# A spectral filter and gated MLP on one core: the late row blocks' last transform as three rounded products, with its operands split one step ahead

## The chip, the cores and the metric

One core of one Trainium2 chip runs one program. The metric is the device time in microseconds. Three runs of the kernel before took 457.14, 457.20 and 456.63 us, median 457.14 us. Besides these there is one profiled execution, whose trace gives the start, the end and the releaser of the instructions on each engine: PE (matrix products; PEld is its loading of stationary operands), DVE and POOL (elementwise), ACT (elementwise and activation functions) and SP, which here issues all the data transfers. Lines such as L956 are those of the kernel before.

## What is computed

The input `x` has 2048 rows of 512 values. Two residual steps follow each other: a filter in the frequency domain, and a gated MLP with 1376 hidden units.

```python
def _A_ref(x, w_r, w_i):                       # global filter
    X = jnp.fft.rfft2(x, axes=(-2, -1)) * (w_r + 1j * w_i)
    return jnp.fft.irfft2(X, s=(S, D), axes=(-2, -1))

def _B_ref(x, w_gate, w_up, w_down):           # gated GELU
    h = gelu(x @ w_gate) * (x @ w_up)
    return h @ w_down

h = x + _A_ref(layernorm(x), w_r, w_i)
out = h + _B_ref(layernorm(h), w_gate, w_up, w_down)
```

All data is 32-bit floating point.

## The kernel before

**The transforms are products.** The 2048 rows are held as 16 row blocks `b` of 128 rows (row 16p + b lies on partition p). The two-dimensional transform is split into products with small constant matrices: over the 128 partitions (`mf`, and `mi` on the way back, kept in SBUF as `mis`), over the 16 blocks (`cf`, `ci`), and over the 512 columns (`df`, `di`). `gh` is the large buffer [128, 16, 512] that holds the spectrum on its way back and then the residual stream `h`. The way back for a block `b` is: over the columns (`over_d_back`, L510, four 128-wide products), a fold of the four column quarters into whole rows (`unfolded`, L805, four POOL instructions of 256 columns, L809 to L812), and then *over the rows*: one product of `mis[:, b]` (128x128) with the block's 512 columns, written to a PSUM bank. The residual `x - mean` is added while the bank is emptied (L957), and the second layer norm's statistics follow (`stats2`, L502).

**Two kinds of products.** A product of two 32-bit operands, as at L956, appears in the trace as two PE records. The MLP instead uses *rounded* operands (type `fp32r`): `split` (L91) writes the rounded value `hi` by an ACT copy (L93) and the rest `lo = full - hi` by a subtraction (L94) on DVE or another engine, and `mm3` (L96) forms hi·hi + hi·lo + lo·hi by three products into one bank (L100, L101, L102).

**The MLP.** Pairs of row blocks are combined so that a 2x2 block product takes seven products instead of eight (`combine`, L530; `products`, L610). Rows come in two halves `q`: blocks 0 to 7, then 8 to 15. For each half the hidden units are walked in eleven *tiles* `n` of 128 units. A tile (`gate_up`, L694) runs the products P0 to P6 into three PSUM banks (banks 0 to 2 or 3 to 5 by the parity of `n`), each of two `mm3`, so six PE products of 512 columns. ACT and DVE empty the banks around them (L651, L654), apply the GELU (L657), multiply gate and up (L660) and split the result into `a` (L666 on ACT for `hi`, L673 on DVE for `lo`). `load_gu` (L127) prepares the next tile's weights: a transfer into `raw`, sums on POOL (L138 to L146), the rounded cast on DVE (L153) and the rests on POOL (L156, three pieces of 256, 768 and 768 columns). `load_d` (L489) does the same for the down weights (L494 on ACT, L496 on POOL). `down` (L732) multiplies `a` with the down weights into banks 6 and 7 (L747), which alternate, and DVE adds each into `gh` (L753, in the last group L750).

**What sets the order.** In the phase `FIRST` (L34, run at L940) the order on PE, ACT, DVE and POOL is written out by hand: blocks 0 to 7 go all the way (`whole`, L814), blocks 8, 9 and 12 (`BY_THEN`) go up to their unfolding, the pairs of the first half are normalised and combined, and tiles 0 and 1 are computed in halves of 256 columns. From tile 2 on (L978) only PE's order is written out. For ACT, DVE, POOL and SP a scheduler places the instructions at build time by a model of time, so an instruction that the source names late may be placed far ahead, among those of `FIRST` too. Each engine then runs its instructions strictly in that order; one that waits holds up all behind it.

**The late blocks.** The generator `late(b)` (L946) has two steps. The first unfolds block `b` on POOL, behind the last L156 (`held("lo")`), except for blocks 8, 12 and 9. The second loads the block's rows of `x`, takes the next of banks 6 and 7, runs the product over the rows on PE (L956), and adds the residual and takes the statistics on DVE. The first step of the blocks listed in `lates` is called near the end of tile `n`: blocks 9 and 13 at tile 2, 10 at tile 3, 14 at tile 4, 11 at tile 5, 15 at tile 6. The second is called in the next tile, after its products P1 and P2. Blocks 8 and 12 get their second step in tile 2.

Of the kernel before, what the change touches and what calls it, by code (L numbers as in the profile page):

```python
# [13 lines left out]
F32R = mybir.dt.float32r  # L14
# [5 lines left out]
S, D, F = 2048, 512, 1376  # L20
P = 128
# [36 lines left out]
def kernel(  # L58
# [15 lines left out]
    nc = tc.nc  # L74
    pe, act, dve, pool = nc.tensor, nc.scalar, nc.vector, nc.gpsimd
# [4 lines left out]
    gh = base.tile([P, NB, D], F32, name="gh")  # L80
# [10 lines left out]
    def split(hi, lo, full, eng=dve):  # L91

        act.activation(hi, full, AF.Copy)  # L93
        eng.tensor_tensor(lo, full, hi.bitcast(F32), op=ALU.subtract)  # L94

    def mm3(o, pairs, onto=False):  # L96

        n = len(pairs)
        for i, ((lh, ll), (rh, rl)) in enumerate(pairs):
            pe.matmul(o, lh, rh, start=(i == 0 and not onto), stop=False, skip_group_check=True)  # L100
            pe.matmul(o, lh, rl, start=False, stop=False, skip_group_check=True)  # L101
            last = pe.matmul(o, ll, rh, start=False, stop=(i == n - 1), skip_group_check=True)  # L102
        return last
# [6 lines left out]
    mis = k3.tile([P, NB, P], F32, name="mis")  # L110
# [12 lines left out]
    def held(k):  # L123

        return tc.issue_after(pooled[k].ins) if k in pooled else ExitStack()

    def load_gu(f, slowly=False, after=None):  # L127

        nonlocal turn
        t = wgp.tile([P, 7, 2 * P], F32, name="raw")  # L130
        nc.sync.dma_start(t[:, :2], wgu[f, :, :2])
        nc.sync.dma_start(t[:, 3:6:2], wgu[f, :, 2:])
        r = gus[:, turn]
        turn = 1 - turn
        gu[f] = r.rearrange("p h m (c n) -> p h m c n", c=2)
        yield
        with held("late"):
            i = pool.tensor_tensor(t[:, 4], t[:, 0], t[:, 3], op=ALU.subtract)  # L138
        if after:
            behind(i, after())  # L140
        yield
        pool.tensor_tensor(t[:, 3], t[:, 3], t[:, 5], op=ALU.add)
        yield
        pool.tensor_tensor(t[:, 2], t[:, 3], t[:, 0], op=ALU.subtract)
        yield
        pool.tensor_tensor(t[:, 6], t[:, 1], t[:, 2], op=ALU.subtract)  # L146
        yield
        if slowly:
            for m in range(7):
                split(r[:, 0, m], r[:, 1, m], t[:, m], pool)  # L150
                yield
        else:
            dve.tensor_copy(r[:, 0], t)  # L153
            yield
            for m in (slice(0, 1), slice(1, 4), slice(4, 7)):
                pooled["lo"] = pool.tensor_tensor(r[:, 1, m], t[:, m], r[:, 0, m].bitcast(F32), op=ALU.subtract)  # L156
                yield
# [328 lines left out]
    w3 = ctx.enter_context(tc.tile_pool(name="w3", bufs=2, reuse_waits="tile"))  # L486
# [12 lines left out]
    def row():  # L499
        return rp.tile([P, D], F32, name="row")  # L500

    def stats2(b):  # L502

        bn = w3.tile([P, 32], F32, name="bn")[:, :6]
        dve.bn_stats(bn, gh[:, b])
        yield
        dve.bn_aggr(mv2[:, b], bn)
        yield
# [92 lines left out]
    def in_turn(i, hns, banks):  # L601

        do = combine(i, hns)
        places = {"T0": ps[:, banks[0]], "T1": ps[:, banks[1]], "s": row(), "e": row()}
        for names in ("T0 a b", "T1 s c d e f g h k", "i j l m n o"):
            for k in names.split():
                do[k](*[places[k]] if k in places else [])
            yield
# [85 lines left out]
    def gate_up(n):  # L694

        do = products(n)[1] if n == 2 else tile_of(n)

        def all_of(names):
            for k in names.split():
                ins = do[k]()  # L700
            return ins

        all_of("P0")
        if n == 2:

            yield
            do = tile_of(n)
            all_of("c1 P1 d1")
        else:
            all_of("c1")  # L710
            yield
            all_of("P1 d1")
        yield
        for names in ("P2 c2", "P3"):
            all_of(names)
            yield
        last = copied[n] = all_of("P4 c3")
        all_of("dy")
        yield

        for _ in load_d(tiles[n][1], last):
            pass

        for names in ("P5", "P6 d2"):
            all_of(names)
            k = names[1] == "6"
            with tc.issue_after(last.ins):
                do[f"G{k:d}"]()
            all_of(f"m{k:d} i{k:d} o{k:d}")
            yield  # L730
# [74 lines left out]
    def unfolded(b, v):  # L805

        s4, v4 = (a.rearrange("p (e h n) -> p e h n", e=2, h=2) for a in (gh[:, b], v))
        u = gh[:, b].rearrange("p (e n) -> p e n", e=2)
        pool.tensor_tensor(v4[:, :, 0], s4[:, :, 0], s4[:, :, 1], op=ALU.add)  # L809
        pool.tensor_tensor(v4[:, :, 1], s4[:, :, 0], s4[:, :, 1], op=ALU.subtract)  # L810
        pool.tensor_tensor(u[:, 0], v[:, :256], v[:, 256:], op=ALU.add)
        pooled["late"] = pool.tensor_tensor(u[:, 1], v[:, :256], v[:, 256:], op=ALU.subtract)  # L812
# [115 lines left out]
    def step(n):  # L928

        if n not in begun_tiles:  # L930
            f = tiles[n][1]
            if f not in gu:
                for _ in load_gu(f):
                    pass
            begun_tiles[n] = gate_up(n)
        next(begun_tiles[n])
# [9 lines left out]
    def late(b):  # L946

        if b not in BY_THEN:

            with held("lo"):  # L950
                unfolded(b, row())
        yield
        xt = row()
        nc.sync.dma_start(xt, x3[:, b])
        py = ps[:, next(bank_67)]
        pe.matmul(py, mis[:, b], gh[:, b], start=True, stop=True)  # L956
        dve.scalar_tensor_tensor(gh[:, b], xt, mv[:, b, 0:1], py, op0=ALU.subtract, op1=ALU.add)  # L957
        for _ in stats2(b):
            pass
        yield  # L960

    def normed(b):

        hn = row()
        act.activation(hn, gh[:, b], AF.Copy, scale=rs2[:, b : b + 1])
        return hn

    def fill(n):
        for _ in range(n):
            next(downs, None)  # L970


    lates = {2: (9, 13), 3: (10,), 4: (14,), 5: (11,), 6: (15,)}
    ending = [late(b) for b in BY_THEN[:2]]
    for g in ending:
        next(g)
    downs = down(0, orders[0][:2], False)
    with tc.manual_schedule(engines={et.PE}):  # L978
        for n, (q, f) in list(enumerate(tiles))[2:]:
            k, at_change = n - q * NF, n == NF - 1  # L980
            if k == 0:
                step(n)
            step(n)
            if k > 8 and not q:
                for i in range(2 * k - 18, 2 * k - 16):
                    with tc.issue_after(copied[n - 1].ins):
                        hns[i] = [normed(b) for b in (8 + i, 12 + i)]
            step(n)
            if at_change:

                steps = [in_turn(i, hns[i], banks) for i, banks in enumerate(((3, 4), (5, 0), (3, 4), (1, 2)))]
                next(steps[0])
            for g in ending:
                next(g)
            if n in (6, 7):

                norm_scales(2 * n - 4, 2)
            fill(2)
            step(n)
            fill(2)  # L1000
            step(n)
            fill(2)

            if k == NF - 1:
                downs = down(q, orders[q][-3:], True)
            if at_change:
                next(steps[0])
                next(steps[1])
            elif k < NF - 1:
                step(n + 1)  # L1010
                fill(2)
            else:
                fill(1)
            ending = [late(b) for b in lates.get(n, ())]
            for g in ending:
                next(g)
            step(n)
            step(n)
            if k in (4, 7):
                downs = down(q, orders[q][: k + 1][-3:], False)  # L1020
            elif k == 1:
                downs = down(q, orders[q][:2], False)
            if at_change:
                gu = {f: gu[f] for f in orders[0][-2:]}
                for s in steps:
                    for _ in s:
                        pass
                    fill(2)
            if k == NF - 1:
                fill(12)  # L1030
# [125 lines left out]
```

## Time and profile before

| what | value |
| --- | --- |
| median of three runs | 457.14 us (456.63 to 457.20) |
| the profiled execution | 456.41 us |
| its span, first to last instruction | 454.6 us |
| PE clock granted | 0.999 |
| instructions in the trace | 6435 |
| packets on the hardware transfer queue | 21136, 40.64 MB |

The profiled execution's own time is 1.8 us above its span. A busy time is the sum of the records of an engine, and PE records overlap: a product of 512 columns has a record of 0.39 us while the next starts 0.23 us later. In the chain of waits the time of a product is what it adds to the chain. In a row of the timeline, the first two numbers are the start in the span and the duration, and the bracket at the end tells how long the engine had been idle and which instruction released it. `x2` or `x12` means that so many equal instructions were merged into one row.

### The profile page before, as it was taken

How to read it: one execution, taken by the hardware profiler on the slowest of the kernel's cores; microseconds unless marked ns; L12 is line 12 of the kernel's file. 1: busy time of each engine (PE TensorE's matmuls, PEld its weight loads, DVE VectorE, ACT ScalarE, POOL GpSimd, SP SyncE). 2: the span in 40 equal slices, each digit the busy share in tenths (PEclk: the TensorE clock that was granted, in tenths of full speed). 3: DMA queues.
4: the chain of work that ended last, by engine and by line, in shares of the span. 5: the costliest groups of instructions: out<-in, count | busy, mean ns of one | idle time of the engine just before them, and what ended most of it. 6: DMA issues, size and time to landing. Idle time of an engine off the chain costs nothing.

```text
span 454.6 us, 6435 instructions
## 1 busy us (share of the span) xinstructions
PE 438.9 (97%) x2289; PEld 371.4 (82%) x2289; DVE 276.9 (61%) x513; ACT 206.6 (45%) x433; POOL 275.5 (61%) x305
## 2 busy tenths in 40 slices
PE   3999998999999999999999999999999999999997
PEld 3899998788967777887888888888888888888876
DVE  5966986797665676358744579256565355535453
ACT  3979876688751233024422776242243024302420
POOL 5985996968868578828752744155566536663210
PEclk9999999999999999999999999999999999999999
DMA  8994804300031122112210203131022102210013
GB/s 253 399 406 132 284 32 156 123 25 1 25 115 47 48 92 92 48 47 71 69 46 25 70 25 128 57 85 55 25 70 69 48 24 71 69 46 25 23 66 121
DMA packets 21168, 41.05 MB, mean 90 GB/s; under 512 B 2064, under 2 KB 7696, under 8 KB 21008
## 3 DMA queue, kind: packets, MB, share of 16 engines
q1 hardware_dynamic: 21136, 40.64, 26.2%
q8 instruction: 18, 0.29, 0.3%
q14 instruction: 14, 0.11, 0.1%
HBM read 36.44 MB, written 4.19 MB: 89 GB/s over the span
## 4 chain that ended last, share of the span: by engine, by line
PE 89%; ACT 4%; DVE 2%; DMA 2%; issue 1%; SPq 1%; DVEq 0%; ACTq 0%
PE ps L747 26%; PE ps L100 15%; PE ps L102 15%; PE ps L101 15%; PE ps L416 3%; PE ps L515 3%; PE ps L427 3%; PE ps L448 2%; PE ps L288 2%; DMA gh<-in_x 2%; PE ps L848 1%; PE ps L956 1%; PE ps L554 1%; ACT ts L293 1%; PE ps L548 1%
## 5 line engine op out<-in xcount | busy, mean ns | idle before, releaser
L100 PE MATMUL ps<-cb,gu 128*128 128x512 f32 (+1 forms) x336 | 127.8, 380 | 2.0 <-ACT s L651 1.6
L747 PE MATMUL ps<-wd,a 128*128 128x512 f32 (+1 forms) x537 | 126.1, 388 | 0.2 <-DVE gh L750 0.2
L102 PE MATMUL ps<-cb,gu 128*128 128x512 f32 (+1 forms) x336 | 124.9, 372 | 0.0
L101 PE MATMUL ps<-cb,gu 128*128 128x512 f32 (+1 forms) x336 | 124.8, 371 | 0.0
L747 PEld LDWEIGHTS ps<-wd,a 128*128 128x128 f32 x537 | 99.2, 188 | 22.4 <-DVE gh L957 0.9
L156 POOL TENSOR_TENSOR gu<-raw,gu 128x768 fp32r<-128x768 f32 (+1 forms) x54 | 78.2, 1476 | 40.0 <-DVE gu L153 38.7
L651 ACT ACTIVATE s<-ps 128x512 f32<-128x512 f32 (+1 forms) x72 | 40.4, 561 | 134.4 <-PE ps L102 134.2
L100 PEld LDWEIGHTS ps<-cb,gu 128*128 128x128 f32 x336 | 63.2, 188 | 15.0 <-ACT s L651 2.2
L101 PEld LDWEIGHTS ps<-cb,gu 128*128 128x128 f32 x336 | 63.2, 188 | 11.7 <-issue 1.0
L102 PEld LDWEIGHTS ps<-cb,gu 128*128 128x128 f32 x336 | 63.2, 188 | 11.1
L753 DVE TENSOR_TENSOR gh<-ps,gh 128x512 f32<-128x512 f32 x48 | 33.0, 690 | 53.5 <-PE ps L747 53.4
L496 POOL TENSOR_TENSOR wd<-wdr,wd 128x512 fp32r<-128x512 f32 x22 | 28.5, 1295 | 51.5 <-ACT wd L494 51.5
L660 DVE TENSOR_TENSOR ps<-ps,s 128x512 f32<-128x512 f32 (+1 forms) x48 | 31.0, 649 | 24.8 <-PE ps L102 22.5
L666 ACT ACTIVATE a<-ps 128x512 fp32r<-128x512 f32 (+1 forms) x48 | 26.9, 561 | 39.0 <-DVE ps L660 38.6
L673 DVE TENSOR_TENSOR a<-ps,a 128x512 fp32r<-128x512 f32 (+1 forms) x48 | 30.7, 640 | 11.8 <-ACT a L666 10.4
L138 POOL TENSOR_TENSOR raw<-raw 128x256 f32<-128x256 f32 x20 | 14.7, 737 | 37.8 <-DMA raw<-in_wgu 36.7
L654 DVE TENSOR_TENSOR s<-ps,s 128x512 f32<-128x512 f32 (+1 forms) x48 | 30.8, 642 | 10.3 <-PE ps L102 8.7
L657 ACT ACTIVATE s<-s 128x512 f32<-128x512 f32 (+1 forms) x48 | 28.2, 592 | 18.4 <-DVE s L654 18.4
L654 DVE TENSOR_TENSOR ps<-ps,s 128x512 f32<-128x512 f32 (+1 forms) x24 | 15.7, 654 | 27.7 <-ACT s L651 27.7
L288 PE MATMUL ps<-ms,pn 128*128 128x128 f32 x120 | 17.6, 297 | 8.3 <-ACT ms L256 8.1
L288 PEld LDWEIGHTS ps<-ms,pn 128*128 128x128 f32 x120 | 16.1, 210 | 8.8 <-POOL pn L263 8.8
L153 DVE CAST gu<-raw 128x1792 fp32r<-128x1792 f32 x18 | 19.6, 1091 | 4.5 <-PE ps L101 2.9
(124 smaller groups left out, 609.7 us busy)
## 6 DMA issues: line engine op xcount, KB each, us to landing
raw<-in_wgu SPq DMA_DIRECT2D x40, 256.0 KB, 3.1
wt<-in_w SPq DMA_DIRECT2D x16, 520.0 KB, 5.4
wdr<-in_wd SPq DMA_DIRECT2D x22, 256.0 KB, 2.6
out<-gh SPq DMA_DIRECT2D x15, 256.0 KB, 2.0
gh<-in_x SPq DMA_DIRECT2D x7, 512.0 KB, 9.6
row<-in_x SPq DMA_DIRECT2D x12, 256.0 KB, 3.0
mis<-in_mi SPq DMA_DIRECT2D x1, 1024.0 KB, 10.7
a<-in_x SPq DMA_DIRECT2D x4, 256.0 KB, 4.3
```

Source lines behind the costliest of these rows:

```text
L100: pe.matmul(o, lh, rh, start=(i == 0 and not onto), stop=False, skip_group_check=True)
L101: pe.matmul(o, lh, rl, start=False, stop=False, skip_group_check=True)
L102: last = pe.matmul(o, ll, rh, start=False, stop=(i == n - 1), skip_group_check=True)
L156: pooled["lo"] = pool.tensor_tensor(r[:, 1, m], t[:, m], r[:, 0, m].bitcast(F32), op=ALU.subtract)
L288: pe.matmul(pt[:, c], o, mc, start=(z == 0), stop=(z == len(parts[b][c]) - 1))
L496: pool.tensor_tensor(r[:, 1], t, r[:, 0].bitcast(F32), op=ALU.subtract)
L651: return lambda: act.activation(to, a, AF.Copy)
L654: return lambda: dve.tensor_tensor(to, a, b, op=ALU.add)
L660: return lambda: dve.tensor_tensor(u, u, g, op=ALU.mult)
L673: dve.tensor_tensor(a[:, 1], u, a[:, 0].bitcast(F32), op=ALU.subtract)
L747: pe.matmul(o, parts_of[tiles.index((q, f))][:, ha, i // 4, r], wds[f][:, hw, c], start=start, stop=stop)
L753: dve.tensor_tensor(gh[:, b, c], o, gh[:, b, c], op=ALU.add)
```

## The change

A step is put between the two steps of `late(b)`: it allocates two tiles from the pool `w3` (two buffers of each), `m` for the two halves of `mis[:, b]` and `v` for those of `gh[:, b]`, and splits both, with an ACT copy and a DVE subtraction each. The product over the rows becomes an `mm3` of these. The main loop calls the new step after a tile's P1, and the product, as before, after its P2. The scratch area that the program reserves for transfers is set to 4096 bytes, where nothing was given before.

```diff
             with held("lo"):
                 unfolded(b, row())
         yield
+        m = w3.tile([P, 2, P], F32R, name="m")
+        v = w3.tile([P, 2, D], F32R, name="v")
+        split(v[:, 0], v[:, 1], gh[:, b])
+        split(m[:, 0], m[:, 1], mis[:, b])
+        yield
         xt = row()
         nc.sync.dma_start(xt, x3[:, b])
         py = ps[:, next(bank_67)]
-        pe.matmul(py, mis[:, b], gh[:, b], start=True, stop=True)
+        mm3(py, [((m[:, 0], m[:, 1]), (v[:, 0], v[:, 1]))])
         dve.scalar_tensor_tensor(gh[:, b], xt, mv[:, b, 0:1], py, op0=ALU.subtract, op1=ALU.add)
...
             if k == 0:
                 step(n)
             step(n)
+            for g in ending:
+                next(g)
             if k > 8 and not q:
...
-    nc = bacc.Bacc("TRN2", target_bir_lowering=False, num_devices=1)
+    nc = bacc.Bacc("TRN2", target_bir_lowering=False, num_devices=1, dynamic_dma_scratch_size=4096)
```

What the scheduler makes of it, in the built program: the order on SP is the same, on POOL one L138 and one L496 change places. The splits of `m` for blocks 8 and 12 stand on ACT behind the last L450 and ahead of the first L830, and on DVE ahead of the first L838, before `FIRST` begins its work. The splits of `v` for blocks 8 and 12 stand inside the end of `FIRST`: on ACT between an L657 and an L666, on DVE between an L654 and an L673. The others stand near their blocks; that of `v` for block 14 is placed on ACT between an L657 and an L651, and on DVE between an L660 and an L673. The splits of `m` for a later block follow the products that free the buffer, which puts them next to the L957 (L962 in the changed kernel) of an earlier block.

## The prediction

> **What bounds the kernel now.** I read the page from the top: busy times, then the chain of waits, then a table of the stretches in which the changed lines run.
>
> ```profile
> span 454.6 us, 6435 instructions
> ...
> PE 438.9 (97%) x2289; PEld 371.4 (82%) x2289; DVE 276.9 (61%) x513; ACT 206.6 (45%) x433; POOL 275.5 (61%) x305
> ...
> PE 89%; ACT 4%; DVE 2%; DMA 2%; issue 1%; SPq 1%; DVEq 0%; ACTq 0%
> 130.00:160.00 30.00, 29.93 (x125) 22.70 (x125) 20.00 (x35) 7.68 (x15) 19.97 (x21) 1.00 0.23 72
> 160.00:190.00 30.00, 30.00 (x130) 24.10 (x129) 17.13 (x28) 9.35 (x17) 24.58 (x28) 1.00 0.25 87
> ```
>
> TensorE is busy 97% of the span and carries 89% of the chain. In the two stretches that hold most of the late row blocks (columns: PE, PEld, DVE, ACT, POOL busy) PE has no gap, DVE is busy half to two thirds of the time, ACT a quarter to a third. So a microsecond of PE work saved there, or of PE waiting added, goes straight into the time. Other engines cost something only where PE, directly or through a queue, waits for them. The clock column stays at 1.00.
>
> **The gain: products.** Per late block, two records of one 32-bit product are replaced by three rounded products.
>
> ```profile
> L956 PE MATMUL ps<-gh,mis 128*128 128x512 f32 x16 | 7.8, 591 | 0.0
> 125.48 0.39 ACT s L651
> 125.92 0.38 PE ps L100
> 134.15 0.76 DVE gh L957
> 134.95 3.06 PE ps L747 x12
> 139.39 3.02 PE ps L747 x12
> 156.00 1.72 PE ps L956 x4
> 157.72 0.23 PE ps L100
> 177.72 0.86 PE ps L956 x2
> ```
>
> Records overlap, so what one adds is read from the chain: 1.72 us for the four of two blocks, 0.43 each, 0.86 a block. A rounded product of this width adds 0.227 (0.23 in the chain; twelve L747 in 2.72 us unstalled). Three add 0.68, so 0.18 is saved per block: 8 x 0.18 = **-1.46 us**. [...]
>
> **The cost: operands.** Each block now issues two copies on ACT (L93: `m` 128x128, `v` 128x512) and two subtractions on DVE (L94).
>
> ```profile
> L494 ACT ACTIVATE wd<-wdr 128x512 fp32r<-128x512 f32 x22 | 13.7, 625 | 8.2 <-PE ps L747 8.2
> L480 ACT ACTIVATE nis<-mis 128x128 f32<-128x128 f32 x2 | 0.5, 300 | 0.0
> L505 DVE BATCH_NORM_STATS2 bn<-gh 128x6 f32<-128x512 f32 x16 | 10.9, 682 | 0.0
> L156 POOL TENSOR_TENSOR gu<-raw,gu 128x768 fp32r<-128x768 f32 x36 | 65.7, 1845 | 0.0
> 14.87 1.26 POOL L263 TENSOR_TENSOR pn<-gh 128x512 f32<-128x512 f32 x1
> 15.14 1.54 DVE L277 TENSOR_TENSOR uv<-pn 128x512 f32<-128x512 f32 x1
> 16.10 1.72 POOL L262 TENSOR_TENSOR pn<-gh 128x512 f32<-128x512 f32 x1
> 29.70 0.42 DVE L277 TENSOR_TENSOR uv<-pn 128x256 f32<-128x256 f32 x1
> 74.22 1.86 POOL L94 TENSOR_TENSOR gu<-raw,gu 128x256 fp32r<-128x256 f32 x2
> 74.34 1.16 DVE L438 TENSOR_TENSOR z<-t,t 128x520 f32<-128x520 f32 x1
> 75.53 0.57 DVE L440 TENSOR_TENSOR z<-z 128x2 f32<-128x2 f32 x1
> ```
>
> ACT: 0.62 + 0.30 a block, 7.4 us over the run, into its idle time. DVE alone would need 0.68 and, on the slope from 0.42 at 256 to 0.68 at 512, some 0.29: 7.8 us. But these read both operands from SBUF, and such a DVE instruction does not run beside a POOL one here. L277 arrives 0.27 into POOL's L263 and ends 0.55 after it (16.68 against 16.13); the POOL instruction behind it then takes 1.72 instead of 1.26. L440, a 2-wide addition right behind L438, takes 0.57, since POOL's second L94 went in between (it ends at 76.08, L440 at 76.10): the two alternate. So a split costs DVE its own 0.55 after the POOL instruction in flight, and POOL about 0.45. POOL instructions are up to 1.85 long and POOL is busy two thirds to four fifths of these stretches.
>
> **Where it decides: the end of the hand-written order.** By the program order, the splits of `v` for blocks 8 and 12 stand on DVE between an L654 and the L673 that follows it; on ACT their copies stand before an L666, and a later L666 waits for that L673.
>
> ```profile
> 123.94 0.42 DVE L654 TENSOR_TENSOR s<-ps,s 128x256 f32<-128x256 f32 x1
> 124.17 2.52 POOL L156 TENSOR_TENSOR gu<-raw,gu 128x256 fp32r<-128x256 f32 x2 [2.16 <-DVE gu L153]
> 124.27 0.41 DVE L673 TENSOR_TENSOR a<-ps,a 128x256 fp32r<-128x256 f32 x1
> 124.72 0.38 ACT L666 ACTIVATE a<-ps 128x256 fp32r<-128x256 f32 x1 [0.30 <-DVE a L673]
> ```
>
> Before, L673 (124.27) releases ACT's L666 (124.72), behind it L657 and L651 (125.48), and that L651 releases PE (125.92, the second row of the chain above). Nothing in it is slack. The two subtractions now come first. POOL's first L156 (0.74; the row's two pieces are 256 and 768 wide) starts at 124.17, 0.10 before the first subtraction can. So: subtraction of 8 ends 124.91 + 0.55 = 125.46; the second L156 goes in between and ends 1.845 - 0.13 later, 127.18 (L262 above ended 1.14 after L277, 0.13 under the 1.27 of its kind); subtraction of 12 ends 127.73; L673 starts 0.09 before that, at 127.64 instead of 124.27. **+3.37 us** for PE at 125.92. What follows hangs on PE, or on ACT's queue behind this L651 (L494, then POOL's L496, L156 and the weight load), so it moves along and pays nothing back. Bounds: +1.2 if the port costs nothing (two steps of 0.60), +1.75 if DVE keeps the port for both, 3.4 if they alternate; I take the last, which L440 shows.
>
> [...]
>
> **The other places** (clock of before, the shift left out).
>
> ```profile
> 136.27 0.74 POOL L146 TENSOR_TENSOR raw<-raw 128x256 f32<-128x256 f32 x1
> 137.05 1.09 DVE L153 CAST gu<-raw 128x1792 fp32r<-128x1792 f32 x1 [0.68 <-POOL raw L146]
> 138.66 1.27 DVE L753 TENSOR_TENSOR gh<-ps,gh 128x512 f32<-128x512 f32 x2
> 161.16 0.70 DVE L654 TENSOR_TENSOR ps<-ps,s 128x512 f32<-128x512 f32 x1 [0.72 <-ACT s L651]
> 175.99 0.76 POOL L812 TENSOR_TENSOR gh<-row 128x256 f32<-128x256 f32 x1
> 177.00 0.69 DVE L660 TENSOR_TENSOR ps<-ps,s 128x512 f32<-128x512 f32 x1
> ```
>
> Tile 2: PE restarts at 139.39 when L753 frees a bank, so DVE sets the pace. New ahead of it are the split of `v` for block 9 and of `m` for 9 and 13, and they hold up POOL's L144 and L146 by 0.45 and 0.2, for whose end (137.01) L153 waits. L153 starts near 138.4; the second L505 now stands ahead of it, so L753 follows 1.0 behind, at 139.4 instead of 138.66. PE is 0.74 late where it should be 0.37 early: **+1.11** (0.2 without the port).
>
> Tile 3: a split of `m` meets the last L156 of 1.85 and the L654 of 161.16 slips to about 162.3, its end to 163.0. PE's product that accumulates onto the same bank (P6) follows 24 products of 0.227 after the 157.72 of the chain, so it starts at 163.0 (a start lies 0.16 before its place in the chain), and at 162.6 once the two blocks' 0.36 are saved: **+0.36** (0 to 1).
>
> Tile 5: block 14 is unfolded by POOL until 176.75, and its first product was issued at 177.56 (0.16 before the chain's 177.72) and is now due 0.18 earlier with block 10's saving. Now the copy must lie between (0.62) and the subtraction behind it, after L660 (177.69) and against POOL's next instructions. With 0.3 for POOL's own delay, the high half is ready at 177.67, the low half at 178.35 to 179.1, the second product's turn is 177.61: **+1.1** (0.7 to 1.5). Behind the copy, which now waits for POOL on ACT, stands the L651 that empties PE's bank; it was not due before 177.8 and loses nothing.
>
> Blocks 10, 11 and 15 have their rows some 4 us ahead or more; their splits fall into DVE's idle time: nothing, at worst 0.5 each. The splits of `m` for 8 and 12 stand between the last L450 and the first L830:
>
> ```profile
> 77.41 0.60 ACT L450 ACTIVATE gh<-ps 128x512 f32<-128x512 f32 x1 [1.11 <-PE ps L448]
> 79.26 0.60 ACT L830 ACTIVATE row<-ps 128x512 f32<-128x512 f32 x1 [1.25 <-PE ps L515]
> q1 hardware_dynamic: 21136, 40.64, 26.2%
> ```
>
> 1.25 us idle on ACT cover 0.6; without that cover it would cost PE the 0.6. SP's order of transfers is unchanged (the load of `row` is issued where it was); on POOL one L138 and L496 change places, for nothing. All data moves through the hardware queue that SP feeds, so the smaller scratch moves addresses and costs nothing.
>
> **Sum**: -1.46 + 3.37 + 1.11 + 0.36 + 1.1 = +4.5 us. The profiled execution took 456.41 us (span 454.6, 1.8 around it), so 460.9; the runs' median is 457.14, 0.7 above it, so **461.6 us**, 460.2 to 463.2 by the bounds of these terms.
>
> **The rivals.**
> - All hidden, the side of a gain: DVE, idle a third of the time, takes the splits in its gaps and only the products show. 457.14 - 1.46 = 455.7. For it: after the L673 of 124.27 DVE has little to do until PE is back. Against: its gaps lie behind that L673, which is what ACT waits for.
> - No port: SBUF subtractions run beside POOL. Then 1.2 at 124, 0.2 in tile 2, 0.6 in tile 5: -1.46 + 2.0 = +0.5, 457.7. Against it L277 and L440.
> - One wait only: DVE keeps the port for both splits, or the first gets it ahead of POOL. 4.5 - 3.37 + 1.75 = +2.9, 460.0. For it: the margin is 0.10 us.
>
> **How the numbers follow.** Forecast 0.56, one wait 0.16, no port 0.13, all hidden 0.15. A measurement tells 0.2% (0.9 us) from no change. Faster 0.15; within 0.2% 0.10 (most of the third case); slower 0.56 + 0.16 + 0.03 = 0.75. The range reaches from below the third case to the top of the first: 457.4 to 463.2; it leaves out the first rival and little above.
>
> **What would show it.** The two L94 of DVE near 124 to 128 with 1.2 and over 2 us instead of 0.68, an L673 behind them near 127.6, PE idle over 3 us before the L100 that stood at 125.92, released by ACT's L651. Three v products per block 0.68 apart from what follows. POOL's L156 lengthened next to L94. PE waits before L747 at the start of tile 2 and before L101 of block 14. I am wrong if the L94 of `v` take 0.68 beside a busy POOL, or if PE has no new gap near 126.

## The result, and the profile after

The changed kernel took 462.47 us (median of 6 runs, 460.15 to 464.32), the kernel before beside it 456.88 us (456.38 to 457.36): 1.0116 times, with a 95% interval of 1.0088 to 1.0143. It is slower by 5.6 us; the forecast was 461.6 us. The profiled execution was the fastest of the six: 460.15 us with a span of 458.4, so the trace explains 3.7 of the 5.6 us.

The page of the changed kernel, its span, busy times and the shares of the chain of waits:

```profile
span 458.4 us, 6478 instructions
...
PE 439.2 (96%) x2297; PEld 374.1 (82%) x2297; DVE 289.6 (63%) x529; ACT 213.0 (46%) x449; POOL 278.3 (61%) x305
...
PE 71%; POOL 12%; ACT 6%; issue 3%; DMA 3%; DVE 3%; SPq 1%; POOLq 0%; ACTq 0%
```

PE is busy 0.3 us longer than before, in a span 3.8 longer. The chain now runs over POOL for 12% (it had no share in the line before), ACT 6 and DVE 3%: waits of other engines have entered it.

The timeline of the changed kernel at the end of the hand-written order, in order of time (start, duration, engine; behind the row, the idle time before it and who ended it):

```profile
124.14 2.95 POOL L156 TENSOR_TENSOR gu<-raw,gu 128x256 fp32r<-128x256 f32 x2 [2.16 <-DVE gu L153]
124.25 3.39 DVE L94 TENSOR_TENSOR v<-gh,v 128x512 fp32r<-128x512 f32 x2
127.56 0.41 DVE L673 TENSOR_TENSOR a<-ps,a 128x256 fp32r<-128x256 f32 x1
128.00 0.38 ACT L666 ACTIVATE a<-ps 128x256 fp32r<-128x256 f32 x1 [3.60 <-DVE a L673]
128.59 0.38 ACT L651 ACTIVATE s<-ps 128x256 f32<-128x256 f32 x1
129.02 0.39 PE L100 MATMUL ps<-cb,gu 128*128 128x256 f32 x1 [3.59 <-ACT s L651]
130.60 0.63 PE L100 MATMUL ps<-cb,gu 128*128 128x512 f32 x1
```

This is the forecast link by link: two subtractions of `v` in 3.39 us instead of 1.2, POOL's two pieces in 2.95 instead of 2.52, L673 at 127.56 (forecast 127.64), and behind it ACT and TensorE. The product that stood at 125.92 starts at 129.02. The last row was not in the forecast: a 512-wide product has a record of 0.63 us instead of 0.39. The table of stretches shows why (columns: PE, PEld, DVE, ACT, POOL busy, then the granted clock, then the DMA share and GB/s):

```profile
128.00:129.00 1.00, 0.00 (x0) 0.00 (x0) 0.42 (x1) 0.99 (x4) 0.00 (x0) 1.00 0.00 0
129.00:130.00 1.00, 0.98 (x7) 0.98 (x8) 0.00 (x0) 0.76 (x2) 0.16 (x1) 1.00 0.00 0
130.00:131.00 1.00, 1.00 (x5) 0.74 (x4) 0.93 (x3) 0.00 (x0) 1.00 (x1) 0.73 0.00 0
131.00:132.00 1.00, 1.00 (x4) 0.68 (x3) 0.60 (x2) 0.00 (x0) 1.00 (x2) 0.50 0.00 0
132.00:133.00 1.00, 1.00 (x7) 1.00 (x6) 0.00 (x0) 0.89 (x3) 0.91 (x1) 0.50 0.54 199
133.00:134.00 1.00, 1.00 (x7) 1.00 (x7) 0.98 (x3) 0.47 (x2) 0.00 (x0) 0.56 0.26 72
134.00:135.00 1.00, 1.00 (x8) 0.91 (x8) 0.85 (x4) 0.73 (x3) 0.00 (x0) 1.00 0.77 219
```

Behind the idle time the granted clock is 0.50 in the slices from 131 to 133 and 1.00 before 130 and behind 134. If it was at one of these two values throughout, 0.73 in one slice and 0.56 in another put the half clock between 130.46 and 133.88, 3.42 us.

**A ruler for the stages.** TensorE's order is the same in all these kernels (a few products are moved in the later ones, 13 are added in one), and up to 22 us behind the first gate product (the first L100 on `cb,gu`) their traces agree to 0.02 us. So each stage can be measured as the start of a TensorE row minus the start of that product, without what lies ahead of it, which differs from execution to execution. Two rows of the timeline of TensorE, kernel after:

```profile
97.86 0.47 PE L100 MATMUL ps<-cb,gu 128*128 128x256 f32 x1
137.16 0.39 PE L100 MATMUL ps<-v,m 128*128 128x512 f32 x1
```

Block 8 starts 137.16 - 97.86 = 39.30 us behind it; before it was 133.03 - 97.89 = 35.14, so +4.16. In the same way, as differences to the kernel before (us; e1 to e9 are the experiments below, "end" is the rest of the span):

| start of | before | after | e7 again | e2 only 8, 12 | e1 8, 12 old | e3 behind | e5 POOL waits | e6 warm | e8 moved |
| --- | --- | --- | --- | --- | --- | --- | --- | --- | --- |
| block 8's products | 35.14 | +4.16 | +4.01 | +4.16 | 0.00 | +0.01 | +1.00 | +3.15 | +0.01 |
| blocks 9 and 13 | 57.95 | +4.22 | +4.39 | +3.66 | +0.32 | +0.36 | +1.66 | +3.72 | -0.45 |
| block 10 | 69.24 | +3.87 | +4.06 | +3.65 | 0.00 | +0.01 | +1.34 | +3.37 | -0.79 |
| block 14's place | 79.67 | +3.85 | +4.04 | +3.65 | -0.03 | -0.02 | +1.29 | +3.33 | -1.02 |
| block 11 | 106.41 | +4.28 | +4.45 | +3.66 | +0.41 | +0.42 | +1.73 | +3.76 | -1.24 |
| block 15 | 116.84 | +4.05 | +4.22 | +3.65 | +0.18 | +0.19 | +1.49 | +3.53 | -1.47 |
| L747 behind block 15 | 127.27 | +3.82 | +4.00 | +3.65 | -0.06 | -0.04 | +1.27 | +3.30 | -1.70 |
| end | 356.71 | +3.83 | +3.99 | +3.68 | -0.08 | -0.04 | +1.32 | +3.24 | -1.74 |
| first gate product at | 97.89 | 97.86 | 98.70 | 100.71 | 101.67 | 99.53 | 99.17 | 99.55 | 98.93 |

How fine the ruler is, two kernels below say that leave these products and splits as they were: e4 and e11 agree with the kernel before up to block 8 and stand 0.14 and 0.17 us under it from tile 2 on, to within 0.06. Both have the smaller scratch, so whether this is the scratch or the spread of the executions is not told. So tile 2 is known to some 0.15 us, the other stages better; the row "end" goes by spans that are printed to 0.1 us.

A block in which nothing is late shows its gain alone: block 11 takes +4.28 to +4.05, block 15 the same step, -0.23 each. Where a step is smaller, the difference is what the place cost. If a block's own first product is late, that shows in the step before it (block 14, below).

### The profile page after: what moved, and what is told of

Its sections match the earlier page's. It is cut to its first block, busy times and chain, and to the rows that moved or that the text cites. A ratio compares the mean times of both kernels' runs of the same rounds, so it can differ in the third digit from the quotient of the medians.

```text
span 458.4 us, 6478 instructions
## 1 busy us (share of the span) xinstructions
PE 439.2 (96%) x2297; PEld 374.1 (82%) x2297; DVE 289.6 (63%) x529; ACT 213.0 (46%) x449; POOL 278.3 (61%) x305
## 4 chain that ended last, share of the span: by engine, by line
PE 71%; POOL 12%; ACT 6%; issue 3%; DMA 3%; DVE 3%; SPq 1%; POOLq 0%; ACTq 0%
PE ps L747 23%; PE ps L100 12%; PE ps L101 12%; PE ps L102 12%; PE ps L288 4%; POOL gu L156 3%; PE ps L515 3%; POOL z L438 2%; ACT dp L420 2%; DMA raw<-in_wgu 2%; DMA gh<-in_x 2%; PE ps L848 1%; DVE v L94 1%; PE ps L554 1%; POOL wd L496 1%
## 5 line engine op out<-in xcount | busy, mean ns | idle before, releaser
L100 PE MATMUL ps<-cb,gu 128*128 128x512 f32 (+1 forms) x336 | 126.6, 377 | 4.9 <-ACT s L651 4.7
L747 PE MATMUL ps<-wd,a 128*128 128x512 f32 (+1 forms) x537 | 125.7, 387 | 0.7 <-DVE gh L753 0.3
L747 PEld LDWEIGHTS ps<-wd,a 128*128 128x128 f32 x537 | 99.3, 188 | 22.0 <-DVE gh L753 0.8
L156 POOL TENSOR_TENSOR gu<-raw,gu 128x768 fp32r<-128x768 f32 (+1 forms) x54 | 78.8, 1488 | 40.0 <-DVE gu L153 37.6
L651 ACT ACTIVATE s<-ps 128x512 f32<-128x512 f32 (+1 forms) x72 | 40.4, 561 | 117.8 <-PE ps L102 117.5
L100 PEld LDWEIGHTS ps<-cb,gu 128*128 128x128 f32 x336 | 63.5, 189 | 17.0 <-ACT s L651 5.3
L496 POOL TENSOR_TENSOR wd<-wdr,wd 128x512 fp32r<-128x512 f32 x22 | 28.5, 1293 | 53.7 <-ACT wd L494 53.7
L666 ACT ACTIVATE a<-ps 128x512 fp32r<-128x512 f32 (+1 forms) x48 | 26.9, 561 | 40.9 <-DVE ps L660 37.3
L660 DVE TENSOR_TENSOR ps<-ps,s 128x512 f32<-128x512 f32 (+1 forms) x48 | 31.0, 650 | 22.9 <-PE ps L102 20.6
L673 DVE TENSOR_TENSOR a<-ps,a 128x512 fp32r<-128x512 f32 (+1 forms) x48 | 30.7, 640 | 12.5 <-ACT a L666 11.2
L138 POOL TENSOR_TENSOR raw<-raw 128x256 f32<-128x256 f32 x20 | 15.2, 760 | 37.0 <-DMA raw<-in_wgu 35.9
L657 ACT ACTIVATE s<-s 128x512 f32<-128x512 f32 (+1 forms) x48 | 28.2, 592 | 19.0 <-DVE s L654 19.0
L654 DVE TENSOR_TENSOR s<-ps,s 128x512 f32<-128x512 f32 (+1 forms) x48 | 30.8, 642 | 9.5 <-PE ps L102 8.0
L654 DVE TENSOR_TENSOR ps<-ps,s 128x512 f32<-128x512 f32 (+1 forms) x24 | 15.6, 652 | 24.1 <-ACT s L651 24.1
L288 PE MATMUL ps<-ms,pn 128*128 128x128 f32 x120 | 17.6, 297 | 8.2 <-ACT ms L256 8.0
L288 PEld LDWEIGHTS ps<-ms,pn 128*128 128x128 f32 x120 | 16.1, 210 | 8.6 <-issue 8.6
L153 DVE CAST gu<-raw 128x1792 fp32r<-128x1792 f32 x18 | 19.6, 1090 | 4.3 <-PE ps L101 3.0
```

The lines of the kernel that those rows point to most:

```text
L288: pe.matmul(pt[:, c], o, mc, start=(z == 0), stop=(z == len(parts[b][c]) - 1))
L496: pool.tensor_tensor(r[:, 1], t, r[:, 0].bitcast(F32), op=ALU.subtract)
L651: return lambda: act.activation(to, a, AF.Copy)
L654: return lambda: dve.tensor_tensor(to, a, b, op=ALU.add)
L660: return lambda: dve.tensor_tensor(u, u, g, op=ALU.mult)
L673: dve.tensor_tensor(a[:, 1], u, a[:, 0].bitcast(F32), op=ALU.subtract)
```

## The experiments

Each was timed beside the kernel before on the same chip; ratios are to that one.

**e1: blocks 8 and 12 as before.**

```diff
+        new = b not in BY_THEN[:2]
+        if new:
...
+            with tc.issue_after(ends["g1bo1"].ins), tc.issue_after(ends["C13"].ins):
+                split(v[:, 0], v[:, 1], gh[:, b])
+            split(m[:, 0], m[:, 1], mis[:, b])
...
+            pe.matmul(py, mis[:, b], gh[:, b], start=True, stop=True)
```

(`ends` holds the last DVE and ACT instructions of the hand-written order; the last line stands for blocks 8 and 12.)

> Blocks 8 and 12 keep the one 32-bit product without a split; the other six blocks are changed (the split of v for block 9 behind the last operations of the hand-written order). My theory, that nearly all of the loss sits at the end of that order: no DVE split between 124 and 128, TensorE back near 125.9 as before, granted clock 1.00 from 126 to 136. Then 6 x 0.18 = 1.1 us of products gained, about 0.55 lost at block 14 and up to 0.4 in tile 2: 456.3 to 457.0 us against some 457 before, and runs no farther apart than those of the kernel before (1 us). Rival, that the loss is spread over all eight blocks (DVE, ACT and the port busier everywhere): six eighths of the 5.6 us stay, 461.

Measured: 457.57 us against 456.79, ratio 1.0008 (0.9992 to 1.0024). In the table there is nothing lost up to block 8, and at the end the trace stands 0.08 below the kernel before. The median is 0.6 us above the range expected, and the runs lie 3.7 us apart, those of the kernel before 4.6. The profiled execution, the slowest of the twelve, reached its first gate product only at 101.67, with a wait of TensorE for L440 (1.5 us) in instructions that are the same in both kernels (below); for the median this explains nothing. The net loss is at blocks 8 and 12; a loss spread over all blocks is out.

**e2: only blocks 8 and 12 changed** (the condition of e1 turned round, no hold).

> Only blocks 8 and 12 are changed, the other six keep the 32-bit product. My theory: the 3.1 us at the end of the hand-written order stay, so does the clock loss behind the long idle time of TensorE (1.0 us in the profiled run of the changed kernel, 3 or more in others), less 2 x 0.18 for products: 460.4 to 463.5 us, with runs 2 to 4 us apart. Rival of a loss spread over the blocks: two eighths of 5.6, 458.3, and runs 1 us apart.

Measured: 462.07 us, ratio 1.0110 (1.0086 to 1.0135), runs 460.85 to 463.57. The trace has the same +4.16 at block 8 as the full change, and keeps +3.68 to the end. Two of eight blocks carry the whole net loss; what the other six gain and what their splits cost nearly cancel (+3.68 against +3.83).

**e3: the two subtractions behind an L673 that comes 7 us later.**

```diff
+        with tc.issue_after(ends["g1bo0"].ins) if b in BY_THEN[:2] else ExitStack():
             split(v[:, 0], v[:, 1], gh[:, b])
```

> All eight blocks changed; alone the DVE subtractions of v for blocks 8 and 12 are held behind an L673 near the end of the hand-written order (131.5 on the clock of before), where POOL is idle. My theory: TensorE's gap at 126 is gone and with it the fall of the clock; both subtractions take 0.68 or less each and are done by 133.0, when the products of block 8 are due (0 to 0.3 late). Sum: -1.46 + 0.55 (block 14) + 0 to 0.4 (tile 2) + 0 to 0.3 = -0.9 to -0.2, 456.0 to 456.8, runs about 1 us apart. Rival, that the clock falls for another reason than the gap: slices under 1.00 between 126 and 140 again and runs 2 to 4 us apart, 458 to 460. Rival of a spread loss: 460 or more.

Measured: 457.06 us against 456.79, ratio 1.0007 (0.9993 to 1.0022), runs 456.16 to 458.58. The timeline of this kernel, on DVE:

```profile
133.46 1.28 DVE L94 TENSOR_TENSOR v<-gh,v 128x512 fp32r<-128x512 f32 x2
134.66 0.68 DVE L654 TENSOR_TENSOR s<-ps,s 128x512 f32<-128x512 f32 x1
```

The same two subtractions take 1.28 us where POOL is idle, and TensorE's gap and the fall of the clock are gone (+0.01 at block 8). The hole is settled by the place of two instructions. But the trace ends only 0.04 below the kernel before, not 0.2 to 0.9, and the median is 0.3 above the range expected: 0.8 us went into tile 2 (+0.36 where two blocks should have gained 0.46) and 0.9 into block 14 (0.2 ahead of its first product, 0.7 behind it).

**e4: the small scratch alone.**

> The kernel before with the smaller DMA scratch alone. My theory: nothing, 456.9 us, within 0.2%. Rival, that moved addresses cost something (bank or partition conflicts of the tiles): a difference of 0.5 us or more in either direction.

Measured: 456.92 us, ratio 1.0001 (0.9980 to 1.0022). It costs nothing that can be seen.

**e5: POOL waits for the second subtraction.** Every engine's order is that of the changed kernel; one dependency is added.

```diff
+    def lo1():
+        next(raw2)
+        behind(pooled["lo"], vs["low"])
```

(`vs["low"]` is block 12's subtraction, `pooled["lo"]` POOL's first L156; the splits of `v` are named in the hand-written order at the places where they already stood.)

> The changed kernel with every engine's order unchanged; added is one wait alone: POOL's first L156 (124.2 us) starts only when DVE's second subtraction of v (block 12) is done, so that POOL is idle beside both. My theory, that DVE and POOL exclude each other and alternate: the two L94 take 0.6 to 0.7 each instead of 3.39 together, L673 stands near 125.5 (127.56 in the changed kernel), TensorE idles 1.7 to 1.9 us instead of 3.59, its clock stays at 1.00, and POOL's later pieces come 1.2 later, inside the 4 us that it waits for its next transfer. From the first gate product to the first product of block 8: 36.35 to 36.5 us (before 35.14, changed kernel 39.30); in all +0.9 to +1.1 by the trace against before, some 457.8 us. Rival, that the subtraction is slow in itself here (operands just written by ACT, rounded output): L94 still 1.7 each, L673 at 127.6, 39.3 us to block 8.

Measured: 458.79 us against 456.62, ratio 1.0046 (1.0029 to 1.0064). Its timeline (L946 is the subtraction here):

```profile
125.55 1.28 DVE L946 TENSOR_TENSOR v<-gh,v 128x512 fp32r<-128x512 f32 x2
126.75 0.41 DVE L673 TENSOR_TENSOR a<-ps,a 128x256 fp32r<-128x256 f32 x1
126.97 2.52 POOL L156 TENSOR_TENSOR gu<-raw,gu 128x256 fp32r<-128x256 f32 x2 [3.67 <-DVE v L946]
```

1.28 against 3.39 us with the same operands, order and neighbours: 2.1 us are the price of POOL's instructions beside them, and POOL's pieces are back to 2.52 from 2.95. The clock stays at 1.00, and block 8 comes at +1.00 instead of +4.16, 0.2 earlier than expected. The end is 0.2 above the expectation, because tile 2 now costs 1.12 (+0.66 from block 8 to blocks 9 and 13 instead of -0.46), where it cost 0.52 in the changed kernel. The median lies 2.2 us above the kernel before, where the trace has 1.3: the 457.8 us expected were missed by 1.0.

**e6: TensorE kept busy while it waits.**

```diff
+        for _ in range(13):
+            pe.matmul(ps[:, 7], w[:, 0, 0, 0], c, start=True, stop=True)
```

> The changed kernel with 13 more 512-wide rounded products (0.227 each, 2.95 us) into an unused PSUM bank, issued just ahead of the product that waits for L651, so that TensorE is busy through most of the 3.59 us. Their results are read by nobody. My theory, that the clock falls because TensorE idled: the wait for L651 stays (the gate product at 129.0), the clock stays at 1.00 behind it, and 38.2 to 38.4 us lie between the first gate product and the first product of block 8 (changed kernel 39.30, before 35.14); in all +2.7 to +2.9 by the trace, and the median over the runs falls by 1 us or more below the changed kernel's, with a smaller spread. Rival, that the fall has another cause (the burst of products behind the wait, the state of the chip): slices of 0.5 to 0.9 after 130 again, 39.3 us.

Measured: 461.17 us against 456.62, ratio 1.0104 (1.0077 to 1.0131). Its table of stretches:

```profile
129.00:130.00 1.00, 1.00 (x5) 0.56 (x3) 0.70 (x2) 0.27 (x1) 0.00 (x0) 1.00 0.00 0
130.00:131.00 1.00, 0.33 (x3) 0.26 (x3) 0.42 (x1) 1.00 (x5) 0.00 (x0) 1.00 0.00 0
131.00:132.00 1.00, 1.00 (x8) 0.93 (x8) 0.25 (x1) 0.49 (x1) 0.43 (x1) 1.00 0.00 0
132.00:133.00 1.00, 1.00 (x5) 0.56 (x3) 0.97 (x4) 0.00 (x0) 1.00 (x2) 1.00 0.00 0
```

The wait is still there, the fall of the clock is not: block 8 comes at +3.15, 1.01 earlier than in the changed kernel. So the idle time caused the fall, and the wait itself is worth 3.15. The granted clock that is listed with each execution says the same: two of these six have 1.00, and none of the 17 of the changed kernel, e2 and e7 has more than 0.996. The second half of the expectation failed: the median is only 0.2 below that of the changed kernel beside it (e7), and the runs lie 3.7 us apart. Tile 2 took back half of the gain (+0.57, so 1.03 lost there; the scheduler set L153 between its two splits of `m` in this kernel). The two longest runs (462.51 and 463.98 us) have a granted clock of 0.993, the two with 1.00 took 460.63 and 461.04: in some executions the clock falls at other places (in the profiled one near 13 us, as it seems: it lists 0.996 though the slices from 125 to 136 have 1.00, and sixteen L288 from 13.66 on take 3.55 us there, 2.02 in the first trace of the changed kernel).

**e7: the changed kernel once more.**

> The changed kernel itself once more, beside the others. My theory: median 461.5 to 463, 3.5 to 6 us above the kernel before. [...]

Measured: 461.38 us against 456.62, ratio 1.0105 (1.0084 to 1.0126). Its table of stretches:

```profile
128.00:129.00 1.00, 0.00 (x0) 0.00 (x0) 0.81 (x2) 0.16 (x1) 0.00 (x0) 1.00 0.00 0
129.00:130.00 1.00, 0.14 (x1) 0.15 (x1) 0.43 (x1) 1.00 (x5) 0.00 (x0) 0.71 0.00 0
...
132.00:133.00 1.00, 1.00 (x4) 0.77 (x4) 0.97 (x3) 0.00 (x0) 1.00 (x1) 0.58 0.04 14
133.00:134.00 1.00, 1.00 (x9) 0.91 (x8) 0.11 (x1) 0.40 (x1) 0.74 (x1) 1.00 0.91 223
```

Here the half clock runs from 129.42 to 132.84, 3.42 us again, but it begins 3.15 us after TensorE went idle (126.27), before the wait is over; in the first trace it was 5.03 (125.43 to 130.46). So the delay was not the same in the two. The difference between the two traces at block 8 is 0.15 us. The median is 0.1 below the range expected.

**e8: the splits moved.** The low parts of `v` for blocks 8 and 12 go to POOL behind its L156, where it waits for a transfer; the splits for blocks 9 and 13 are held behind the last copy of tile 2; block 14's products come one part later in tile 5.

```diff
+        with held("lo") if b in BY_THEN[:2] else tc.issue_after(copied[2].ins) if b in (9, 13) else ExitStack():
+            split(v[:, 0], v[:, 1], gh[:, b], pool if b in BY_THEN[:2] else dve)
...
-            for g in ending:
-                next(g)
+            if n != 5:
+                for g in ending:
+                    next(g)
             if n in (6, 7):
...
             fill(2)
+            if n == 5:
+                for g in ending:
+                    next(g)
             step(n)
```

> The changed kernel with its splits moved: the low parts of v for blocks 8 and 12 on POOL, where it waits for a transfer (129.8 to 133.8 before); the splits for blocks 9 and 13 held behind the last copy of tile 2; block 14's products one part later in tile 5. My theory, that the products gain 0.23 a block (blocks 11 and 15 in the traces) and that the rest of the loss was lateness of splits: -1.84 for the products, 0 at the end of the hand-written order, at most 0.5 left in tiles 2 to 5: -1.8 to -1.3 by the trace from the first gate product on, 455.0 to 455.6 us. Rival, that DVE's work for the splits costs PE its banks wherever it is put: +0.3 to +0.8 in tile 2 or 3 for what was 0.5 at its start, and no gain over the kernel before.

Measured: 455.63 us against 456.62, ratio 0.9978 (0.9961 to 0.9995). Each block now shows close to its gain (last column of the table): -0.45 for blocks 8 and 12, -0.34 for 9 and 13, about -0.23 for each of the four others, -1.74 in all. The rival, that DVE's splits cost PE its banks wherever they stand, is out.

**e9: the low parts of `m` for 8 and 12 on POOL as well** (the edit against e8, in part).

```diff
-            if b in (9, 13):
-                split(m[:, 0], m[:, 1], mis[:, b])
+            if b in (8, 12, 9, 13):
+                split(m[:, 0], m[:, 1], mis[:, b], pool if b in BY_THEN[:2] else dve)
```

> As e8_moved, and the low parts of m for blocks 8 and 12 on POOL too, next to those of v, instead of on DVE near 78 us. My theory, that these two operations near 78 us are hidden: no change beyond 0.3 us against e8_moved, 455.3 to 455.9. Rival, that they hold up POOL's L866 and with it TensorE's L848 near 81 us (waits of 0.2 and 0.5 us on L866 in two traces of changed kernels, none before): 0.3 to 0.8 less than e8_moved, 454.9 to 455.3, and no wait of L848 on L866 in the trace.

Measured: 455.69 us against 457.55, ratio 0.9956 (0.9934 to 0.9978), -1.78 by the trace. POOL's stretch in the timeline:

```profile
130.37 1.30 POOL L94 TENSOR_TENSOR v<-gh,v 128x512 fp32r<-128x512 f32 x1
131.64 0.46 POOL L94 TENSOR_TENSOR m<-mis,m 128x128 fp32r<-128x128 f32 x1
132.06 1.30 POOL L94 TENSOR_TENSOR v<-gh,v 128x512 fp32r<-128x512 f32 x1
133.32 0.45 POOL L94 TENSOR_TENSOR m<-mis,m 128x128 fp32r<-128x128 f32 x1
134.35 0.74 POOL L138 TENSOR_TENSOR raw<-raw 128x256 f32<-128x256 f32 x1 [0.58 <-DMA raw<-in_wgu]
```

All four fit between the last piece and the transfer, with 0.58 us to spare. The median lies in the range of the theory that the two operations are hidden. This version is 0.4% faster than the kernel before.

**e10: e8 once more.**

> e8_moved itself once more, for a narrower interval: 455.0 to 456.0 us, 0.1 to 0.35% below the kernel before.

Measured: 456.41 us against 457.55, ratio 0.9966 (0.9942 to 0.9989), -1.71 by the trace. The median misses the absolute range by 0.4, but the kernel before stood 0.9 higher than beside e8; the ratio holds. Against e9 on the same chip it is 0.7 slower, with intervals that overlap.

**e11: the kernel before with the split of `m` for 8 and 12 added, and unused.**

```diff
+        if b in BY_THEN[:2]:
+            m = w3.tile([P, 2, P], F32R, name="m")
+            split(m[:, 0], m[:, 1], mis[:, b])
```

> The kernel before with the small DMA scratch and the split of m for blocks 8 and 12 alone near 78 us; nobody reads the halves, the products are the old ones. My theory (hidden): 456.6 to 457.1, the same as before within 0.2%, and 19.8 to 20.1 us from the first L515 behind the last L448 to the first gate product (before 19.83, scratch alone 20.08). Rival (they push L866): 20.2 to 20.7 us there, and a median 0.3 to 0.8 above the kernel before.

Measured: 456.97 us, ratio 0.9993 (0.9975 to 1.0011). The median is the same, but the trace has 21.11 us from L515 to the first gate product, above both ranges, and this among TensorE's waits:

```profile
PE ps L448 <- POOL z L440: 1.5, 1, 1.5
PE ps L848 <- POOL row L866: 1.0, 1, 1.0
```

The wait on L866 occurs in six of the ten traces that have the subtractions of `m` near 78 us (0.2, 0.5, 0.6, 0.2, 0.3, 1.0) and in none of the three that have none there (before, e4, e9). That looks like the rival of e9, but the timeline of this kernel, on DVE and POOL, speaks against it:

```profile
79.87 0.49 DVE L94 TENSOR_TENSOR m<-mis,m 128x128 fp32r<-128x128 f32 x2 [3.22 <-ACT m L93]
83.11 0.72 POOL L138 TENSOR_TENSOR raw<-raw 128x256 f32<-128x256 f32 x1 [4.84 <-DMA raw<-in_wgu]
83.79 1.41 POOL L866 TENSOR_TENSOR row<-row 128x256 f32<-128x256 f32 x2
```

The subtractions are over at 80.36, while POOL waits until 83.11 for the transfer of its L138; L866 stands behind that one, and starts 0.7 us after it in all thirteen traces. TensorE's wait goes by when L138 starts behind the first L515: no wait at up to 2.35 us, 0.2 to 0.3 at 2.56 to 2.62, 0.5 and 0.6 at 2.90 and 2.94, 1.0 at 3.42. So the wait is that of a late transfer, and no trace shows a path from the splits to it.

## Why the prediction was right, step by step

The time (462.5 against 461.6) and the place were right, and the terms partly made up for one another. That the median came so close is partly luck: the forecast added 0.7 us from the profiled execution to the median, and here they lie 2.3 apart, while the trace itself is 0.7 us below the sum. By the table, the profiled execution's +3.83 splits into:

| term | forecast | measured in the trace |
| --- | --- | --- |
| products, 8 blocks | -1.46 | -1.84 (8 x 0.23) |
| end of the hand-written order, the wait | +3.37 | +3.13 (129.02 - 97.86 against 125.92 - 97.89) |
| the clock behind it | not in the sum | +1.03 (4.16 - 3.13) |
| tile 2 | +1.11 | +0.52 (+0.06 instead of -0.46) |
| tile 3 | +0.36 | +0.11 |
| block 10 | 0 | 0 |
| tile 5, block 14 | +1.1 | +0.87 (+0.41 from block 10 to block 11 instead of -0.46) |
| sum | +4.48 | +3.82 |

- **The wait at 126 us was right in mechanism and size.** e1, e2 and e3 put the loss on the two subtractions of `v` for blocks 8 and 12; e5 shows that 2.1 of their 3.39 us are POOL's share, as the alternation worked out from L440 and L263 said: one after the other they take 1.18 and 2.28. What the forecast calls the port is no more than this in the traces: the pair took 3.39 us beside POOL and 1.28 without it (e3, e5), and no run shows what lies behind it. The 0.24 less than forecast are in part a slack that the prediction denied: from L666 to L651 ACT now takes 0.59 (128.00 to 128.59), before 0.76. The L94 of `v` in the groups of the changed kernel (duration in ns: least, median, greatest) show it over all eight:

```profile
L94 DVE TENSOR_TENSOR v<-gh,v x8: 692/1054/2284, 124.2 to 215.6; 128x512 fp32r<-128x512 f32 x8
```

  The rivals fall with it: if POOL beside them cost nothing, all would be at 692, and "one wait only" would have left L673 at 126, not 127.56.
- **"What follows moves along and pays nothing back" was the step that left the clock out.** The forecast stated that TensorE would idle more than 3 us and gave that time no consequence. Behind it TensorE ran at a granted clock of 0.50 for 3.42 us, and block 8 lost another 1.03 (0.89 in e7: 4.01 - 3.12). e6 shows that the idle time is the cause: filled, the same wait costs 3.15 and no more. In the two traces the clock was halved for 3.42 us each time, from 3.15 us (e7) and 5.03 us (after) behind the start of the same wait; what sets the length and the delay, no run shows.
- **Tile 2 had the right mechanism; its size depends on when TensorE arrives.** The splits there, in the timeline of the changed kernel (first) and of e5:

```profile
139.02 0.74 POOL L146 TENSOR_TENSOR raw<-raw 128x256 f32<-128x256 f32 x1
139.38 0.93 DVE L94 TENSOR_TENSOR v<-gh,v 128x512 fp32r<-128x512 f32 x1
140.83 0.47 DVE L94 TENSOR_TENSOR m<-mis,m 128x128 fp32r<-128x128 f32 x2
```

```profile
137.54 0.99 DVE L94 TENSOR_TENSOR v<-gh,v 128x512 fp32r<-128x512 f32 x1
139.05 1.03 DVE L94 TENSOR_TENSOR m<-mis,m 128x128 fp32r<-128x128 f32 x2
139.20 0.74 POOL L146 TENSOR_TENSOR raw<-raw 128x256 f32<-128x256 f32 x1
```

  In e5 both meet POOL, as forecast, and the tile costs 1.12 (forecast 1.11). In the changed kernel TensorE, slowed by the clock, was a microsecond later against POOL: L146 had ended (139.76) before the splits of `m`, and the tile cost 0.52, with 0.84 in e7, where the split of `v` took 1.18. The two splits together last 0.6 us longer in e5 (2.02 against 1.40), which is the difference. So part of the clock's loss was probably taken back here. e8 shows that the place decides: behind the last copy of tile 2 the same splits cost about 0.1.
- **Tile 3 came almost free.** With the tile's shift of 4.22 taken off, L654 slipped by 0.7 us instead of 1.1 and ended (166.72) 0.11 before the P6 that adds to its bank (166.83), so TensorE did not wait as forecast. Half of the +0.11 is that two blocks back to back gained 0.41, not 0.46; P6's second product came 0.05 late.
- **Tile 5 had the right mechanism at 0.87 instead of 1.1.** The changed kernel's timeline of the chain, from POOL over ACT and DVE to TensorE:

```profile
179.91 0.75 POOL L812 TENSOR_TENSOR gh<-row 128x256 f32<-128x256 f32 x1
180.69 0.63 ACT L93 ACTIVATE v<-gh 128x512 fp32r<-128x512 f32 x1 [0.68 <-POOL gh L812]
180.95 0.39 PE L102 MATMUL ps<-cb,gu 128*128 128x512 f32 x1
181.38 0.50 PE L100 MATMUL ps<-v,m 128*128 128x512 f32 x1
181.36 0.69 DVE L94 TENSOR_TENSOR v<-gh,v 128x512 fp32r<-128x512 f32 x1
182.10 0.50 PE L101 MATMUL ps<-v,m 128*128 128x512 f32 x1 [0.22 <-DVE v L94]
```

  The copy waits for POOL's unfolding, the first product for the copy, the second for the subtraction. The first starts 0.43 us behind the product before it instead of 0.23, so 0.2 are lost ahead of it; in the table that stands in the step from block 10 to block 14's place, and 0.66 in the next. POOL's next instruction (L138) had started 0.75 us earlier and did not hold the subtraction up: 0.69, the low end of the range given. e8 takes the cost away by calling the product later.
- **A block alone gained 0.23, not 0.18.** By this its pair of 32-bit records cost TensorE 0.68 + 0.23 = 0.91, an estimate, 0.05 more than the 0.86 read from the chain. That is four times 0.227, so the saving is about the time of one rounded product.
- **"The splits of `m` near 78 us are hidden"** was right as far as the runs tell: ACT still stands idle for 0.85 us ahead of L830 (1.25 before), and the waits of TensorE there are those of a transfer (e11).
- **The scratch** cost nothing that can be seen (e4: ratio 1.0001).

**What stays open.** Median and profiled execution differ by 2.3 us for the changed kernel. Part of that goes with the clock. By estimate, a stretch of 3.42 us at half clock takes 0.0037 off the mean granted clock of an execution (half of 3.42 in 458), and the clocks listed with the executions of the changed kernel lie near multiples of it (0.996, 0.992 and 0.993, 0.988 and 0.989). The profiled one has 0.996, the fall behind the wait alone; the five others have 0.988 to 0.993, by this estimate one or two falls more. Of the 17 executions of the changed kernel, e2 and e7, 13 have more than one fall by this count; of the 75 of the kernel before beside the experiments, 25 have any, and they took longer with each (beside e1: 456.62 us in the median of the 22 without, 457.52 with one, 460.42 in the only one with two). As far as the traces place them, the further falls lie ahead of the first gate product, which the thirteen profiled executions reach between 97.86 and 101.67 us: near 13 us in e6, e7 and e11, where sixteen L288 took 3.44 to 3.55 us (2.02 in the first trace of the changed kernel), and near 78 us in e1, with a mean clock of 0.86 from 74 to 80 us and 0.78 from 80 to 84. The profiled executions of e1 and e2 list 0.991 and 0.988, which by the estimate leaves at least one fall more in each. The rest is known in part: near 75 us DVE's L438 and L440 meet POOL's pieces, and TensorE waits for L440 between 0 and 1.5 us from one execution to the next, in instructions that the change does not touch. Whether the changed kernels have more such falls and waits than the kernel before by more than chance, and why, was not settled.

## What to carry over

An operation that is short and has time to spare costs what it holds up where the scheduler puts it: look up the instruction behind it in its queue, and who waits for that one. Two subtractions of SBUF operands on DVE took 1.28 us with POOL idle (e5) and 3.39 beside POOL (the changed kernel), so they should be costed with what POOL has in flight; the cheapest place for them here was POOL itself while it waited for a transfer (1.30 us each in e9, hidden). The wait of 3.59 us on TensorE cost 0.9 to 1.0 us more by the half clock behind it; the wait of 1.48 us in the same place in e5 brought no half clock.

## What was not expected of the hardware

- The granted clock fell to one half for 3.42 us after a wait of 3.59 us, in every trace of the changed kernel with that wait (after, e2, e7), and began while TensorE was still idle in one of them (e7); with the wait down to 1.5 us (e5: TensorE idle from 126.73 to 128.21) or filled (e6) it stayed at 1.00 from 125 to 136 us. At half clock the 512-wide rounded products followed each other at 0.43 us (e2: 132.92, 133.35, 133.78) instead of 0.23.
- The fall cost 0.9 to 1.0 us at block 8, less than half of the 3.42 us, 1.7, which is the author's estimate of the work that the half clock left undone.
- Executions ran within 0.02 us of each other for 22 us behind the first gate product, yet reached that product up to 3.8 us apart, with nearly the same instructions ahead of it; in e6, e7 and e11 sixteen L288 near 13 us took 3.44 to 3.55 us, behind waits of TensorE of 2.55 to 2.73 us; in the first trace of the changed kernel, e5, e8, e9 and e10 they took 2.02 behind waits of 1.28 to 2.03 us.
